# Linear attention and a highway layer on one core: 64-row turns, unequal score and state groups, 512-column feed-forward, buffers behind a pad, a new order

## The chip, the cores and the metric

The kernel runs on one core of one Trainium2 chip. A core has a matrix engine (TensorE, PE in the profile), three engines for elementwise work (VectorE or DVE, ScalarE or ACT, GpSimd or POOL), and SyncE (SP), which here only issues DMAs. TensorE reads SBUF and writes the eight banks of PSUM; the other engines move results from PSUM to SBUF. The metric is the device time of one execution in microseconds (us), lower is better.

## What is computed

Inputs are q, k, v of 4 batches x 8 heads x 768 positions x 64, a decay `lam` per head, and a highway layer (two 512x512 matrices, one bias). First comes linear attention with decay; its output, 3072 tokens of 512 features, goes through the layer.

```python
# attention, per batch and head, in blocks of 64 positions
intra = (qb @ kb.T * Dmask) @ vb            # Dmask[i, j] = lam ** (i - j) for i >= j, else 0
inter = (qb * lam_pow) @ kv_state           # lam_pow[i] = lam ** (i + 1)
out   = intra + inter
kv_state = lam ** 64 * kv_state + (kb * rev_pow).T @ vb
...
# highway layer on x = out, tokens by 512
H = np.maximum(x @ w_h, 0.0)
T = 1.0 / (1.0 + np.exp(-(x @ w_t + b_t)))
return T * H + (1.0 - T) * x
```

The kernel scales q by lam to the power of the position and v by its inverse, so that the decay needs no mask of its own and the state no rescaling: inside a chunk only a triangle of ones is left. T*H + (1-T)*x is computed as x + T*(max(H, 0) - x).

## The kernel before

**Units.** The work is cut into twelve pairs n = 0 to 11 of 2 x 128 positions, three for each batch; a pair has chunks b = 0 and 1 of 128 positions. Positions 2p and 2p+1 lie in partition p (J = 2), so that a DMA row is 512 bytes; a chunk is then one half of the partitions. Heads are handled two at a time (hp = 0 to 3, e = 0 or 1 within).

**An order written out by hand.** `PLAN` is a string of tokens, each of which issues one step. The order of tokens is the order in each engine's queue; the engine stands behind `@`, the PSUM bank behind `=`. Each engine works its queue in order, and the semaphores between engines follow from the tiles. The first pairs' tokens:

```python
Lk.0.0 Lv.0.1 Lv.0.0 Lq.0.0 Lk.0.1 Lq.0.1 Lv.1.1 CK.0.0@POOL Lq.1.0 Z.12=0 TK.0.0=0 Lq.1.1 CV.0.0@DVE Lk.1.0
CQ.0.0@POOL EK.0.0@DVE Lv.1.0 CV.0.1@DVE CK.0.1@ACT Lk.1.1 Z.11=1 TQ.0.0=1 B=2 EQ.0.0@ACT CQ.0.1@POOL W.0.1 W.0.0
```

**The steps of a pair**, with token, function and line:

1. `Lk`, `Lq`, `Lv` load half the heads of k, q or v, 256 KB (L178); `W` loads half a weight matrix, rows of 2 KB (L182). All come from SP's queue, and so do the stores. Five buffers each hold k, q and v.
2. `CK` casts k to bf16 (L102 or L100), `CQ` and `CV` scale q and v by the powers of lam (L195), mostly on POOL.
3. `TK`, `TQ` turn k and q on TensorE, eight turns of 128x128 each (L209), into one bank each. `EK`, `EQ` evacuate them; EQ also interleaves the two positions of a partition (`c j`), so that q stands in the order of positions.
4. `SS` issues, for one e, 16 score matmuls (64x64 tiles, 128 columns, L222) in turn with 16 state matmuls (64 columns, L227). `KE` copies the state out of PSUM. `M` multiplies 512 elements of scores by the triangle on VectorE (L261).
5. `I` (inter, state times q, full array, L277) and `A` (intra, masked scores times v, 64x64 tiles, L287) add up in one bank for each chunk. `D` takes the sum to SBUF as bf16, feature by token: the feed-forward's input xT.
6. `F` is one feed-forward block: eight matmuls of 256 columns (L305), half the output features of one matrix for one pair. A pair has four: u = 0, 1 for w = 0 (H) and w = 1 (T). `H` computes max(H, 0) - x on VectorE (L310), `G` the sigmoid on ScalarE in two instructions of 256 columns (L319), in place in PSUM, `X` the gate on VectorE (L323).
7. `R` adds x and the gated part and turns the sum to token by feature, with 32 matmuls of 64x128 tiles against the identity (L352). `E` copies it to SBUF, `ST` stores 512 KB from SP's queue (L361). The last pair goes in two groups of 128 tokens, with full-array turns (L332) and stores in pieces (L342).

`Z` issues matmuls of 512 columns that nobody reads (spins, L371), to raise TensorE's clock and hold it while data is awaited. `B` and `BC` turn the bias to a column. Before the plan, lam is loaded to all 128 partitions, and its logarithm and powers are computed (L126 to L133). Small tiles (lam_bc, bt_r, id128, blank, tri, the powers and others) are allocated ahead of the weights and the load buffers.

The feed-forward's blocks are independent of the next pairs' attention, so the plan puts them between the attention's steps.

## Time and profile before

| | |
|---|---|
| median of 3 runs | 109.11 us (108.94 to 109.52) |
| span of the profiled execution, first to last instruction | 107.8 us |
| median less span | 1.3 us |
| mean granted TensorE clock | 0.992 |
| read from HBM, written | 20.98 MB, 6.29 MB |
| packets of the load queue | 42528 |

The profile is one execution. A page gives the busy time of each engine, the span in 40 slices, the DMA queues, the chain of work that ended last, the costliest groups and the DMA issues; other views give groups by form, waits, the chain in order of time, windows and the timeline. In a group, "out<-in" are tiles, a leading b marks a PSUM bank, and the last column is the idle time before the instructions with what ended it. Busy time of matmuls includes their latency, so the chain is the better source for their price: there, each piece reaches to the start of the next. Durations below are rounded as the views give them.

### The profile page before, as it was taken

The numbers are of one execution on the slowest core, as the hardware profiler recorded it, in microseconds if no ns is written. First come the engines' busy times: TensorE is split into PE (matmuls) and PEld (weight loads), VectorE is DVE, ScalarE is ACT, GpSimd is POOL, SyncE is SP. The second block draws the span as 40 slices with busy tenths as digits, with TensorE's granted clock in tenths as the row PEclk, the third lists the DMA queues.
The fourth block names the chain that finished last, engine by engine and source line by source line (L and its number), as shares of the span: only waits on it lengthen the run. The fifth ranks groups of instructions, "written<-read, shape, count | busy, mean of one in ns | idle before, by whom it ended". The sixth has DMA issues, their size and how long they took to land.

```text
span 107.8 us, 4970 instructions
## 1 busy us (share of the span) xinstructions
PE 100.5 (93%) x2190; PEld 81.0 (75%) x2190; DVE 83.4 (77%) x140; ACT 70.1 (65%) x129; POOL 55.6 (52%) x46
## 2 busy tenths in 40 slices
PE   4998999999999999999999999999999899999950
PEld 1333655488987888889889889889898688899940
DVE  1053495879699987999995997999977978958860
ACT  2213347485875588499669758957697778587940
POOL 6028342127889887985468593999770600000000
PEclk9999999999999999999999999999999999999996
DMA  1799999999999999999999999999979334108264
GB/s 29 191 304 289 292 356 389 324 292 266 288 288 263 312 295 291 276 291 281 292 298 285 272 360 309 306 289 342 355 220 317 141 138 158 43 6 316 79 239 150
DMA packets 42701, 27.59 MB, mean 256 GB/s; under 512 B 1588, under 2 KB 38712, under 8 KB 42680
## 3 DMA queue, kind: packets, MB, share of 16 engines
q1 hardware_dynamic: 42528, 27.27, 86.7%
q8 instruction: 17, 0.28, 1.1%
q14 instruction: 4, 0.03, 0.1%
q10 hardware_dynamic: 152, 0.01, 0.1%
HBM read 20.98 MB, written 6.29 MB: 253 GB/s over the span
## 4 chain that ended last, share of the span: by engine, by line
PE 74%; DVE 10%; DMA 5%; issue 3%; POOL 1%; SPq 1%; ACT 1%; POOLq 0%; DVEq 0%
PE bt L305 18%; PE bh L305 17%; PE bs L222 7%; PE bx L352 6%; PE bo L287 6%; DMA qf<-in_q_dram 5%; DVE m L261 5%; PE bqtr L209 5%; PE bspin L371 5%; PE bktr L209 4%; PE bo L277 3%; DVE hm L310 2%; DVE th L323 2%; PE kv L227 2%; POOL qb L195 1%
## 5 line engine op out<-in xcount | busy, mean ns | idle before, releaser
L305 PEld LDWEIGHTS <-w_b 128*128 128x128 bf16 x416 | 36.4, 98 | 5.3 <-issue 0.9
L261 DVE TENSOR_TENSOR m<-bs,tri 128x512 bf16<-128x512 f32 x48 | 31.1, 683 | 2.8 <-PE bs L222 2.6
L195 POOL TENSOR_TENSOR qb<-qf,pow_q 128x1024 bf16<-128x1024 f32 (+1 forms) x13 | 23.5, 1810 | 9.4 <-DMA qf<-in_q_dram 8.7
L319 ACT ACTIVATE bt<-bt,bt_col 128x256 f32<-128x256 f32 (+1 forms) x52 | 22.0, 432 | 7.9 <-PE bt L305 4.4
L305 PE MATMUL bt<-xT,w_b 128*128 128x256 bf16 (+1 forms) x208 | 24.5, 265 | 0.7 <-issue 0.5
L305 PE MATMUL bh<-xT,w_b 128*128 128x256 bf16 (+1 forms) x208 | 25.0, 265 | 0.0
L195 POOL TENSOR_TENSOR vs<-vf,pow_v 128x1024 bf16<-128x1024 f32 x10 | 19.0, 1903 | 8.8 <-DMA vf<-in_v_dram 6.4
L310 DVE SCALAR_TENSOR_TENSOR hm<-bh,xT 128x512 bf16<-128x512 f32 (+1 forms) x26 | 16.5, 644 | 3.3 <-PE bh L305 2.4
L323 DVE TENSOR_TENSOR th<-bt,hm 128x512 bf16<-128x512 f32 (+1 forms) x26 | 16.5, 644 | 2.1 <-ACT bt L319 2.0
L371 PE MATMUL bspin<-blank,id 128*128 128x512 bf16 x45 | 13.4, 447 | 1.4 <-POOL id masks.py:199 1.4
L222 PE MATMUL bs<-qT,kT 64*64 64x128 bf16 x384 | 13.9, 218 | 0.4 <-PE bspin L371 0.2
L100 ACT ACTIVATE ss<-kv 128x512 bf16<-128x512 f32 x15 | 9.0, 597 | 7.5 <-PE bs L222 6.3
L102 POOL CAST kb<-kf 128x1024 bf16<-128x1024 f32 (+1 forms) x10 | 9.9, 994 | 6.0 <-DMA kf<-in_k_dram 6.0
L222 PEld LDWEIGHTS <-kT 64*64 64x64 bf16 x384 | 10.9, 106 | 2.6 <-issue 1.1
L100 ACT ACTIVATE xT<-bo 128x512 bf16<-128x512 f32 x16 | 9.2, 597 | 4.4 <-PE bo L287 4.4
L100 ACT ACTIVATE o<-bx 128x512 f32<-128x512 f32 x19 | 10.5, 596 | 1.3 <-PE bx L352 1.3
L100 ACT ACTIVATE qT<-bqtr 128x1024 bf16<-128x1024 bf16 (+1 forms) x10 | 9.8, 980 | 1.8 <-PE bqtr L209 1.8
L371 PEld LDWEIGHTS <-id 128*128 128x128 bf16 x45 | 4.5, 110 | 7.1 <-issue 2.8
L287 PE MATMUL bo<-m,vs 64*64 64x128 bf16 x384 | 9.1, 219 | 0.4 <-DVE m L261 0.4
L227 PE MATMUL kv<-vs,kb 64*64 64x64 bf16 x320 | 9.3, 196 | 0.0
L100 ACT ACTIVATE kT<-bktr 128x1024 bf16<-128x1024 bf16 (+1 forms) x7 | 6.8, 970 | 2.1 <-PE bktr L209 2.1
L287 PEld LDWEIGHTS <-vs 64*64 64x64 bf16 x384 | 6.5, 106 | 2.1 <-issue 1.2
(50 smaller groups left out, 111.1 us busy)
## 6 DMA issues: line engine op xcount, KB each, us to landing
kf<-in_k_dram SPq DMA_DIRECT2D x24, 256.0 KB, 5.3
vf<-in_v_dram SPq DMA_DIRECT2D x24, 256.0 KB, 5.3
qf<-in_q_dram SPq DMA_DIRECT2D x24, 256.0 KB, 5.7
out_dram<-o SPq DMA_DIRECT2D x11, 512.0 KB, 4.8
w_f<-in_moe_w_h_dram SPq DMA_DIRECT2D x2, 512.0 KB, 6.0
w_f<-in_moe_w_t_dram SPq DMA_DIRECT2D x2, 512.0 KB, 8.4
out_dram<-oh SPq DMA_DIRECT2D x2, 128.0 KB, 2.0
out_dram<-oq SPq DMA_DIRECT2D x1, 256.0 KB
```

The source lines that it names most:

```text
L100: A.activation(dst, src, AF.Copy)
L102: ENG[eng].tensor_copy(dst, src)
L195: ENG[eng].tensor_tensor(dst, in0=get(src, n)[:, heads(p)].rearrange("p h (j d) -> p h j d", j=J), in1=pw[:, n % NST, heads(p), :, None].t ...
L222: T.matmul(get("s", n, e, hp // 2)[half(b), hp % 2, j, :], lhsT=get("kT", n)[half(e), hp, j, half(b)], rhs=get("qT", n)[half(e), hp, b * C ...
L227: T.matmul(kv[half(e), hp, half(e)], lhsT=get("kb", n)[half(b), j, 2 * hp + e, :], rhs=get("vs", n)[half(b), 2 * hp + e, j, :], start=firs ...
L261: V.tensor_tensor(new(("m", n, e, u), [128, 2, J, C]), in0=get("s", n, e, u), in1=tri[:, None].to_broadcast([128, 2, J, C]), op=ALU.mult)
L287: T.matmul(get("o", n, b)[half(e), hp, :], lhsT=get("vs", n)[half(b), 2 * hp + e, j, :], rhs=get("m", n, e, u)[half(b), hp % 2, j, :], sta ...
L305: T.matmul(t[:, r, :], lhsT=w_b[w][:, kc, (2 * u + r) * 128:(2 * u + r + 1) * 128], rhs=get("xT", *g)[:, kc, :], start=(kc == 0), stop=(kc ...
L310: V.scalar_tensor_tensor(new(("hm", g, u), [128, 2, z * C], tag=f"hm{z}"), in0=get("h", g, u), scalar=0.0, in1=get("xT", *g)[:, 2 * u:2 * ...
L319: A.activation(dst[:, r, :], src[:, r, :], AF.Sigmoid, bias=bt_col[:, 2 * u + r:2 * u + r + 1])
L323: ENG[eng].tensor_tensor(new(("th", g), [128, NP, z * C], tag=f"th{z}")[:, 2 * u:2 * u + 2, :], in0=get("tt", g, u), in1=get("hm", g, u), ...
L371: T.matmul(t, lhsT=id128, rhs=blank, start=True, stop=True)
```

## The change

- **Turns.** k and q of a pair are turned in 64-row pieces, each chunk into a bank of its own that holds k and q (`turn_kq`, tokens `TK.n.x.p`, x = 0 for k and 1 for q); an evacuation takes one chunk, k and q together or one of them (`evac_kq`, token `E`). The interleave moves from q to the evacuation of the attention output (`take`), and the triangle is laid out accordingly.
- **Scores.** For each e, 8 scores stand with 16 states (`SU`), and the other 16 scores of both e in a step of their own (`S`).
- **Feed-forward.** `GROUPS` gives the groups: pairs 0, 1 and 10 alone (256 columns), 2+3, 4+5, 6+7, 8+9 together (512 columns), and the two chunks of pair 11 alone (128). A block has one PSUM bank of 512 columns; a group of 512 has eight blocks, four for each matrix. The sigmoid of such a block is one instruction. With `@POOL` it writes to SBUF and POOL computes the gate (13 of 25), with `@DVE` it stays in PSUM.
- **lam** is loaded as one row; its logarithm is spread over the partitions by a matmul (`powers`). The bias's turn is the first token.
- **Buffers** are all allocated at the start, behind a tile of 384 bytes, and each has a multiple of 512 bytes. Load buffers are six instead of five, output buffers three instead of five.
- **Order.** The plan is new. Weights are loaded in halves of columns (rows of 1 KB), the first behind 18 loads of q, k and v, where before it stood behind 12; three stores instead of five stand ahead of the last load. Pair 11's turns follow pair 10's directly. Spins are 26 instead of 45. The last pair's chunks come last, one stored in two pieces of 128 KB, the other as 256 KB.

```diff
+GROUPS = [[(0, 0), (0, 1)], [(1, 0), (1, 1)], [(2, 0), (2, 1), (3, 0), (3, 1)], [(4, 0), (4, 1), (5, 0), (5, 1)], [(6, 0), (6, 1), (7, 0), (7, 1)], [(8, 0), (8, 1), (9, 0), (9, 1)], [(10, 0), (10, 1)], [(11, 0)], [(11, 1)]]
...
+B=0 L.0.0.0 L.1.0.0 L.1.0.1 Z.3.512=1 PW=1 CQ.0.1@POOL L.2.0.1 Z.7.512=2 TK.0.1.1=12 PT L.0.0.1 CK.0.0@ACT TK.0.0.0
...
+D.0.0@DVE SU.1.1=6 W.0.1 W.1.1 KE.1.0@ACT WC.0.1.1@POOL E.2.1.1@ACT M.1.1.0 M.1.0.1 Z.3.512=4 SU.1.0=1 I.1=64 L.1.3.1
...
+CQ.11.2@POOL S.9=51 M.9.1.1 M.9.0.1 D.8.0@ACT D.8.1@ACT TK.10.0.2=46 L.2.11.0 TK.10.1.2 CK.11.2@POOL KE.9.0@ACT
+TK.11.0.2=12 TK.11.1.2 E.11.0.2@ACT E.10.1.2@DVE E.10.0.2@DVE CV.10.2@POOL SU.9.0=5 KE.9.1@ACT M.9.0.0 ST.3.2.2
...
+R.11.1.0=56 X.8.0.1@DVE H.7.0.2 R.11.1.1=03 ER.11.1.1.1@ACT ER.11.1.0.0@ACT ER.11.1.1.0@ACT ST.11.1.1 X.7.0.2@DVE
+ER.11.1.0.1@DVE ST.11.1.0 R.11.0.2=40 ER.11.0.2.1@ACT ER.11.0.2.0@DVE ST.11.0.2
...
-BUFS = dict(kf=5, qf=5, vf=5, kb=3, qb=2, vs=3, kT=2, qT=2, m=8, xT4=2, th4=2, xT2=3, xT1=2, th2=2, th1=2, hm2=3, hm1=2, tb2=2, tb1=2, ss=4, o=5, oh=2, oq=1)
+BUFS = {'kf': 6, 'qf': 6, 'vf': 6, 'o': 3, 'oh': 1, 'oq': 2, 'kb': 3, 'qb': 2, 'vs': 3, 'kq': 3, 'm': 10, 'ss': 4, 'hm': 3, 'tb': 3, 'x128': 2, 'x256': 2, 'x512': 2, 't128': 2, 't256': 2, 't512': 2}
...
-    lam_bc = singles.tile([128, H], F32)
-    A.dma_start(out=lam_bc, in_=lam.partition_broadcast(128))
+    pad = singles.tile([128, 96], F32)
+    ln_r = pad[0:1, 0:H]
+    bt_col = pad[:, 8:8 + KC]
...
+    for tag in BUFS:
+        for i in range(BUFS[tag]):
+            kept[tag, i] = singles.tile(*SHAPES[tag], name=f"{tag}_{i}_")
...
+    A.dma_start(out=lam_r, in_=lam.rearrange("(o h) -> o h", o=1))
...
+    def powers(bk):
+        ln = bank(("ln",), bk[0], [128, H])
+        T.matmul(ln, lhsT=ones, rhs=ln_r, start=True, stop=True)
+        V.tensor_tensor(p_ln, in0=ln[:, None, :, None].to_broadcast([128, NST, H, J]),
+                        in1=tk_f[:, :, None, :].to_broadcast([128, NST, H, J]), op=ALU.mult)
+        A.activation(pow_q, p_ln, AF.Exp)
+        A.activation(pow_v, p_ln, AF.Exp, scale=-1.0)
...
-    def load_w(w, g):
-        nc.sync.dma_start(out=w_f[w][:, 2 * g:2 * g + 2],
-                          in_=(moe_w_h, moe_w_t)[w][256 * g:256 * g + 256].rearrange("(kc p) m -> p kc m", p=128))
...
+    def load_w(w, c):
+        cs = slice(256 * c, 256 * c + 256)
+        nc.sync.dma_start(out=w_f[w][:, :, cs], in_=(moe_w_h, moe_w_t)[w][:, cs].rearrange("(kc p) m -> p kc m", p=128))
...
+    def turn_kq(n, x, p, bk):
+
+        for b in range(2):
+            bank(("kqt", n, b), bk[b] if bk else 0, [128, 2, NP, J, Q], BF16)
+        for hp in range(NP) if p == 2 else (2 * p, 2 * p + 1):
             for j in range(J):
-                T.transpose(t[:, i, j, :], get(x + "b", n)[:, j, h:h + 2, :], id128)
...
+                for b in range(2):
+                    T.transpose(get("kqt", n, b)[:, x, hp, j, :], get(("kb", "qb")[x], n)[half(b), j, 2 * hp:2 * hp + 2, :],
+                                id128[half(b), half(b)])
+
+    def evac_kq(n, b, x, eng):
+
+        xs = slice(0, 2) if x == 2 else slice(x, x + 1)
+        copy(eng, new("kq", n)[:, b, xs], get("kqt", n, b)[:, xs])
...
     def scores_state(n, e, bk):
...
+        bank(("s", n, e, 0), bk[0], [128, 2, J, J, Q])
+        with_state = e == 1 or n % NST != NST - 1
+        for i, (hp, j) in enumerate(PJ[:4]):
+            for b in range(2):
+                score(n, e, hp, j, b)
+            if with_state:
+                for hp, j in PJ[2 * i:2 * i + 2]:
+                    for x in range(2):
+                        state(n, 1 - e, hp, j, x)
...
     def take(n, b, eng):
...
+        g, at = place[n, b]
+        copy(eng, new(f"x{width[g]}", g)[:, :, at:at + C].rearrange("p n (c j) -> p n j c", j=J),
+             get("ob", n, b).rearrange("p n (j c) -> p n j c", j=J))
...
+    def block(g, u, w, bk):
+        z = width[g]
+        r = 512 // z
+        t = bank(("HT"[w], g, u), bk[0], [128, r, z])
+        for i in range(r):
             for kc in range(KC):
...
+                T.matmul(t[:, i, :], lhsT=w_b[w][:, kc, (r * u + i) * 128:(r * u + i + 1) * 128],
+                         rhs=xt(g)[:, kc, :], start=(kc == 0), stop=(kc == KC - 1))
...
+    def sigm(g, u, p, eng):
...
+        if eng == "POOL":
+            made["S", g, u] = new("tb", g, u).rearrange("p (r z) -> p r z", z=z)
+        else:
+            made["S", g, u] = t
+        for i in range(s.start, s.stop):
+            A.activation(get("S", g, u)[:, i, :], t[:, i, :], AF.Sigmoid, bias=bt_col[:, r * u + i:r * u + i + 1])
...
+    def gate(g, u, p, eng):
...
+        ENG[eng].tensor_tensor(new(f"t{z}", g)[:, r * u + s.start:r * u + s.stop, :], in0=get("S", g, u)[:, s],
+                        in1=get("hm", g, u).rearrange("p (r z) -> p r z", z=z)[:, s], op=ALU.mult)
...
-    def spin(r, bk, idle=[0]):
+    def spin(r, z, bk, idle=[0]):
```

## The prediction

> **What bounds the kernel now.** I read the page first, then the chain, the waits, the windows by stage and the groups by form. The page gives the busy shares, the slices and the chain:

> ```profile
> span 107.8 us, 4970 instructions
> ## 1 busy us (share of the span) xinstructions
> PE 100.5 (93%) x2190; PEld 81.0 (75%) x2190; DVE 83.4 (77%) x140; ACT 70.1 (65%) x129; POOL 55.6 (52%) x46
> ...
> PE   4998999999999999999999999999999899999950
> ...
> DMA  1799999999999999999999999999979334108264
> ...
> PE 74%; DVE 10%; DMA 5%; issue 3%; POOL 1%; SPq 1%; ACT 1%; POOLq 0%; DVEq 0%
> ```

> TensorE is full from the second slice to the 38th and holds 74% of the chain. But a second row is as full: the DMA engines up to slice 31. The waits and the timeline of POOL say what that means:

> ```profile
> POOL qb L195 <- DMA qf<-in_q_dram: 8.7, 7, 2.1
> POOL vs L195 <- DMA vf<-in_v_dram: 6.4, 3, 4.1
> POOL kb L102 <- DMA kf<-in_k_dram: 6.0, 5, 3.0
> ```
> ```profile
> 84.43 1.90 POOL L195 TENSOR_TENSOR vs<-vf,pow_v 128x1024 bf16<-128x1024 f32 x1 [4.08 <-DMA vf<-in_v_dram]
> ```

> POOL waits for loads until the last V, 84.4 us into the span. TensorE has some 2 us of other work when each pair of chunks lands; a TensorE that gets faster by several us runs into the loads. So two paths have to be summed: TensorE's own, and the load stream. The windows give the stream's rate (columns: length, busy of each engine, clock, DMA share, GB/s):

> ```profile
> 14.00:20.00 6.00, 5.53 (x107) 3.28 (x101) 4.50 (x7) 3.20 (x4) 1.93 (x3) 1.00 1.06 375
> 20.00:58.00 38.00, 37.76 (x907) 32.32 (x900) 33.48 (x54) 27.98 (x50) 27.06 (x18) 1.00 1.07 288
> ```

> In 20 to 58 us only q, k and v move, in rows of 512 bytes: 288 GB/s. In 14 to 20 us nearly all is weights, in rows of 2 KB: 375 GB/s. With 16 engines a row of 512 bytes takes 16x512/288 = 28.4 ns and one of 2 KB 87.4 ns, so 512 bytes more cost 19.7 ns and each row has a fixed 8.8 ns.

> **The change on TensorE.** Prices come from the chain (start, us, what):

> ```profile
> 15.91 1.74 PE bspin L371 x8
> ...
> 34.00 0.57 PE bx L352 x32
> 34.58 0.55 PE bqtr L209 x8
> 35.13 0.87 PE bt L305 x8
> ...
> 40.21 0.45 PE bktr L209 x8
> ...
> 41.75 0.57 PE bo L287 x32
> ```

> Eight turns of 128 rows take 0.45 us after other full-array work and 0.55 after 64-row work: a full matmul of 128 columns is 56 ns, and a change between full, 64x128 and 64x64 tiles about 0.10 us (0.093 by the unrounded starts). Thirty-two 64-row matmuls take 0.57 with one such change, so 0.47, or 14.7 ns each, both for 64x128 (L352) and for 64x64 tiles (L287). A matmul of 256 columns is 0.87/8 = 109 ns, one of 512 columns 1.74/8 = 217 ns, and two of the first are one of the second.

> - Turns: 192 full ones (10.8 us) become 384 of 64 rows; their form, 64 rows by 128 with 64 columns, is that of L352, so 384 x 14.7 ns = 5.6 us: 5.1 less.
> - Scores and states: the same 384 and 320 matmuls, in groups of 24 and 16: 10.9 becomes 10.6.
> - Feed-forward: the same columns, in matmuls of 512 for four groups: 42.1 becomes 41.8. Eight steps instead of four for twice the tokens is no gain in itself.
> - Output turns 6.1 becomes 5.6; inter 4.5 and intra 5.4 stay.
> - Tile changes: counted along both plans, 59 become 68: 5.5 becomes 6.3, as each 64-row turn now interrupts full-array work.

> Together 85.3 us of needed TensorE work becomes 80.1. What stands behind the first feed-forward block falls from 79.2 to 72.2, since pair 2 is turned and scored ahead of it now (work ahead of it: 6.1 becomes 7.9, beside the spins, 45 becoming 26, which lie in time that waits for data anyway).

> The same sum against the trace of before:

> ```profile
> 5.65 0.61 POOL L102 CAST kb<-kf 128x512 bf16<-128x512 f32 x1 [3.00 <-DMA kf<-in_k_dram]
> ...
> 22.24 1.91 PE L305 MATMUL bh<-xT,w_b 128*128 128x256 bf16 x16
> ```
> ```profile
> 104.34 0.42 DVE L102 COPY oh<-bx 128x256 f32<-128x256 f32 x1 [0.44 <-PE bx L332]
> ```

> From 22.2 to 104.3, where the last copy gets its data from TensorE, are 82.1 us for 79.2 of work: 2.9 of stalls. Behind that come 3.5 us of evacuation and store.

> **The other engines.** These rows price them (groups by form of VectorE, ScalarE and POOL; then the load of lam, with its time to landing):

> ```profile
> L261 DVE TENSOR_TENSOR m<-bs,tri 128x512 bf16<-128x512 f32 x48 | 31.1, 683 | 2.8 <-PE bs L222 2.6
> ...
> L102 DVE COPY kT<-bktr 128x1024 bf16<-128x1024 bf16 x5 | 3.4, 685 | 1.2 <-PE bktr L209 1.1
> L102 DVE CAST ss<-kv 128x512 bf16<-128x512 f32 x5 | 3.4, 681 | 0.0
> L102 DVE COPY qT<-bqtr 128x1024 bf16<-128x1024 bf16 x2 | 2.4, 1224 | 0.4 <-PE bqtr L209 0.4
> ```
> ```profile
> L319 ACT ACTIVATE bt<-bt,bt_col 128x256 f32<-128x256 f32 x44 | 19.5, 449 | 7.7 <-PE bt L305 4.4 <-ACT xT L100 1.8 <-ACT o L100 0.8
> L100 ACT ACTIVATE o<-bx 128x512 f32<-128x512 f32 x19 | 10.5, 596 | 1.3 <-PE bx L352 1.3
> ```
> ```profile
> L195 POOL TENSOR_TENSOR qb<-qf,pow_q 128x1024 bf16<-128x1024 f32 x11 | 20.9, 1902 | 7.1 <-DMA qf<-in_q_dram 6.4 <-PE bx L352 0.7
> ...
> L195 POOL TENSOR_TENSOR qb<-qf,pow_q 128x512 bf16<-128x512 f32 x2 | 2.6, 1303 | 2.3 <-DMA qf<-in_q_dram 2.3
> L102 POOL CAST w_b<-w_f 128x512 bf16<-128x512 f32 x3 | 1.8, 625 | 5.8 <-DMA w_f<-in_moe_w_h_dram 3.4 <-DMA w_f<-in_moe_w_t_dram 2.5
> ```
> ```profile
> lam_bc<-in_lam_dram ACTq DMA_DIRECT2D x1, 4.0 KB, 4.4
> ```

> - VectorE: the interleave leaves the turned q (1224 against 685 ns) for the evacuation of the attention output, which reads 4-byte PSUM at 683 ns in any order (as the masks and the state copies do). Thirteen gates go to POOL, some output and state evacuations change sides with ScalarE. Counted along the plan, about 82 us against 83.4.
> - ScalarE: 16 sigmoids of 512 columns at about 0.60 (the row of o) replace two of 0.45 each: 22 becomes 17.6; copies and casts of k take that up: about 68.
> - POOL: 13 gates of 128x512, which the trace does not show on POOL. Ends: 0.95 (half the 1902 row) and 1.30 (the mean of two of 512 elements). I take 1.04, nearer to the half, which has 11 instances behind it. 55.6 becomes about 63.
> - Behind the first block VectorE has 68.5 us, ScalarE 58, POOL 51.5 against TensorE's 72.2. But up to pair 6 it is VectorE 35.4 and POOL 32.6 against 34.9: no slack there. One evacuation now takes k and q of a chunk together, so it waits for the later of the two, as a rule POOL's scaling of q, 1.9 us behind its load; the masks and gates queued behind it on VectorE wait with it, and TensorE's intra part for those. I put the stalls at 3.5 us, 0.6 over those of before: less than one such wait of 1.9, as the plan puts feed-forward blocks between.
> - lam as a row: the first scalings of q waited 2.3 us for their data and not for the powers, so nothing is won. Deeper load buffers (six instead of five) win nothing by themselves either: the DMA share is over 1 already. The bias turn is first in TensorE's queue now and everything there waits for its small load, up to about 5 us; the lam load, its neighbour, took 4.4. Only spins stand behind it: nothing, at most 1 us.

> **The load stream.** The new pad of 384 bytes stands first, and every buffer behind it has a multiple of 512 bytes; before, small tiles of 3584 bytes in sum (seven times 512) stand there with no such pad, so if the pad brings the buffers onto a 512-byte boundary, all load buffers lie 128 bytes past one now. No row of the trace has an aligned transfer. The bounds: nothing (28.4 ns a row, 288 GB/s), or the whole fixed part (19.7 ns); the fastest stage seen, 375, lies between. I take half, 24 ns or 340 GB/s; the other rows at 375. (The weights come in rows of 1 KB now; between the two, 0.1 us each.)

> [...]

> The first block waits for the first half of one weight matrix, which now stands behind 18 loads (4.72 MB) instead of ahead of most of pair 2: 5.65 (the first load, above) + 4.46/0.340 + 0.52/0.375 + two casts of 0.625 on POOL = 21.4 us. At 288 it is 23.8.
> The last k half stands behind 18.6 MB of loads and 3.67 MB of weights and stores (three stores of 0.52 instead of five ahead of it): 5.65 + 18.35/0.340 + 9.8 = 69.4 us. Its cast takes 1.0, and from the last turns on TensorE has 26.2 us left.
> The end: behind the last block come relu and gate (0.68 each, as a mask), 16 turns (0.24) and a copy of 0.42, with about 0.1 from engine to engine 2.5 us; 0.6 of it (the turns that the plan has there) is in TensorE's sum already. Then a store of 256 KB instead of 128: 3.0 us follow the copy at 104.34 (which ends at 104.76) up to 107.8, and 128 KB more are 0.35 at 375 GB/s. Together 5.3 us behind TensorE's sum, where before had 3.5.

> **Sums.** TensorE's path: 21.4 + 72.2 + 3.5 + 5.3 = 102.4. Load path: 69.4 + 1.0 + 26.2 + 5.3 = 101.9. They are as good as equal, and the first sets the end. Median 109.11 less the span 107.8 leaves 1.3 around it: **103.7 us**, 5% less than before.

> **Rivals.**
> - *The loads run no faster.* Then the load path decides: 5.65 + 63.7 + 9.8 + 32.5 = 111.7, and 113.0 us: slower, since the new order puts all of pair 11's turns late and together. It decides against the change below 307 GB/s (18.35/r = 107.8 - 47.95). For it: rows of 512 bytes run at 288 now, and their fixed part may have nothing to do with where they start. Against: 2 KB rows show that neither memory nor engines are at their limit at 288.
> - *VectorE and POOL take over up to pair 6.* With gates at 1.30 to 1.56 POOL gets 2 to 3 us more work there than fits, and in-order queues hand it on: stalls of 7, 107.2 us. For it: VectorE is busy 33.5 of 38 us in the window from 20 to 58. Against: before had 34.8 of 36.3 there too, with 2.9 of stalls in all.
> - *The 64-row turns don't overlap* (the change doesn't do what it says): 29 ns each instead of 14.7, 5.6 us back: 109.3. Against it: L352's pairs with the same shape.
> - *Loads as fast as the weights*, 375: the first block at 20.2, 102.5, or 101 with fewer stalls.

> **Chances.** Forecast 0.60 (its own range 101.5 to 106), loads unchanged 0.15, VectorE and POOL 0.15, turns 0.05, faster loads 0.05. The range 101.0 to 109.6 leaves out the first rival and little else; half-way loads (307 to 325 GB/s) lie in it. About 0.5% is what a measurement of this kernel can tell from no change. Faster: forecast, VectorE/POOL and fast loads, 0.78 with what falls off at their edges; same: half of the turns and an edge of VectorE, 0.04; slower: the loads and half of the turns, 0.18.

> **What would show it.** In the profile after: a window with q, k and v alone at about 340 GB/s, not 288; the DMA row falling off near slice 27 of 40; turns of 16 in about 0.24 us; first block near 21.4; POOL's waits on loads no longer than now; TensorE's last matmul near 99. Wrong it would be if the last casts of k and v wait for DMA past 75 us, if POOL's gates take over 1.3, or if TensorE idles on masks and gates for over 5 us.

## The result, and the profile after

The kernel takes 114.64 us (median of four runs, 113.97 to 117.33) against 109.31 before on the same chip: a ratio of 1.0431, 95% interval 1.0341 to 1.0521. It is 4% slower; 103.7 us, and faster, was forecast. Ratios, and the single times given below, leave out disturbed runs, which were 2 to 7 us longer and up to three of the four of one kernel (in e4 two of four, 114.73 and 114.85 us); the traces of e2 and e8 are of such runs.

The page of the kernel after, profiled at 113.97 us:

```profile
span 112.3 us, 5101 instructions
PE 94.8 (84%) x2253; PEld 62.8 (56%) x2253; DVE 80.6 (72%) x137; ACT 68.1 (61%) x116; POOL 65.0 (58%) x58
...
PE   0699879849999999999899986299999999999920
...
PEclk9999999995999999999999999959999999999996
DMA  2999999999999999999999999993200000081783
...
q8 instruction: 17, 0.28, 1.0%
...
PE 69%; DVE 10%; issue 7%; DMA 7%; ACT 3%; ACTq 0%; DVEq 0%
```

TensorE was 93% of the span and is 84%. The loads end at slice 27, as forecast. VectorE, ScalarE and POOL came out at 80.6, 68.1 and 65.0 us, against 82, 68 and 63 forecast. New are two holes in TensorE's row (slices 9 and 25 to 26), two 5s in the granted clock just behind them, and "issue", time in which an engine waits for nothing that the profile shows: 7% of the chain instead of 3%.

The windows after (same columns as before):

```profile
14.00:20.00 6.00, 5.02 (x164) 3.30 (x163) 4.62 (x10) 4.10 (x9) 5.09 (x7) 1.00 1.09 327
20.00:58.00 38.00, 35.02 (x868) 24.46 (x868) 30.83 (x51) 26.88 (x42) 29.13 (x22) 0.96 1.06 314
```

The loads run at 314 GB/s: above 288, below 340. A tenth of that is weights, in rows of 1 KB; from 32 to 56 us, where q, k and v are alone, it is 307 (289 before). TensorE loses 3 of 38 us where it lost 0.2. The chain says at what:

```profile
22.14 1.73 issue
23.88 0.22 PE bs L233
24.19 0.23 PE bob L302 x14
24.42 1.20 PE bH L328 x8
25.61 3.20 PE bT L328 x16
...
60.48 0.57 PE bkqt L224 x32
...
68.37 1.06 PE bot L372 x61
69.43 2.92 issue
72.35 0.23 PE bot L372 x3
72.58 1.55 PE bH L328 x4
74.13 1.71 PE bT L328 x4
75.84 1.13 PE bH L328 x4
```

Read the long stop first. It stands between the 61st and the 62nd of 64 output turns (pairs 4 and 5, L372). The three turns behind it read the same two buffers, write the same banks and run on the same engine as those ahead; no data can be missing. The stop at 22.14 is of the same kind, within a group of scores and states. Behind both, feed-forward matmuls run at half speed for a while: four of 512 columns take 1.55 and 1.71 us instead of 0.87, sixteen of 256 take 3.20 instead of 1.74. That is where the clock row has its 5s (granted clock 0.50 from 25.1 to 28.4 and from 72.9 to 76.2 us); the two places cost some 1.8 us each.

Counted in the trace in order of start, a weight load and a matmul for each of the 2253, such stops stand ahead of instructions 700, 2236, 2748 and 3004 (from 0): 1536, 512 and 256 apart, all multiples of 256. The instruction queue of the DMA (q8 above) moved 17 packets of 16 KB for these 4506 instructions, which fits 256 to a packet. From the start of the last matmul ahead of a boundary of 256 to that of the first behind it are, over all boundaries, 7.3 us in sum (1.93, 0.19, 0.85, 0.74 and 3.11, and small ones in which TensorE doesn't stop), against 1.3 before the change; the idle time alone is 5.8 us (1.73, 0.64, 0.52 and 2.92).

The packets' times tie the two together. In the trace after, TensorE goes on 1.44, 1.49, 1.36 and 1.34 us after a packet of the instruction queue has landed. At every boundary where the packet had landed 1.69 us ahead or more, there is no stop. A packet's transfer starts 0.7 to 3.4 us after TensorE has crossed the boundary before, and in one case 0.46 us ahead of it.

### The profile page after: what moved, and what is told of

It is laid out like the page before. It is cut to its first block, busy times and chain, and to the rows that moved or that the text cites. A ratio compares the mean times of both kernels' runs of the same rounds, so it can differ in the third digit from the quotient of the medians.

```text
span 112.3 us, 5101 instructions
## 1 busy us (share of the span) xinstructions
PE 94.8 (84%) x2253; PEld 62.8 (56%) x2253; DVE 80.6 (72%) x137; ACT 68.1 (61%) x116; POOL 65.0 (58%) x58
## 4 chain that ended last, share of the span: by engine, by line
PE 69%; DVE 10%; issue 7%; DMA 7%; ACT 3%; ACTq 0%; DVEq 0%
PE bT L328 18%; PE bH L328 16%; PE bs L233 8%; PE bspin L401 7%; PE bob L302 5%; DMA out_dram<-o__87 5%; PE bot L372 5%; PE bkqt L224 4%; PE bob L292 4%; DMA bt_r<-in_moe_b_t_dram 2%; PE kv L238 2%; DVE hm__119 L339 2%; DVE hm__118 L339 2%; ACT bT L352 1%; DVE m__109 L272 1%
## 5 line engine op out<-in xcount | busy, mean ns | idle before, releaser
L328 PEld LDWEIGHTS <-w_b 128*128 128x128 bf16 x288 | 25.2, 102 | 16.1 <-issue 2.8
L352 ACT ACTIVATE bT<-bT,pad 128x128 f32<-128x128 f32 (+2 forms) x20 | 9.3, 469 | 12.1 <-PE bT L328 6.3
L328 PE MATMUL bT<-x__127,w_b 128*128 128x512 bf16 x32 | 9.1, 412 | 0.0
L328 PE MATMUL bH<-x__127,w_b 128*128 128x512 bf16 x32 | 8.9, 410 | 0.0
L401 PE MATMUL bspin<-blank,id 128*128 128x512 bf16 x26 | 8.8, 454 | 0.0
L328 PE MATMUL bH<-x__128,w_b 128*128 128x512 bf16 x32 | 8.1, 379 | 0.0
L328 PE MATMUL bT<-x__128,w_b 128*128 128x512 bf16 x32 | 8.0, 380 | 0.0
L107 ACT ACTIVATE x__128<-bob 128x512 bf16<-128x512 f32 x8 | 5.7, 751 | 1.6 <-PE bob L302 1.4
L233 PE MATMUL bs<-kq__102 64*64 64x128 bf16 x128 | 4.4, 221 | 1.7 <-issue 1.7
L233 PE MATMUL bs<-kq__101 64*64 64x128 bf16 x128 | 4.8, 220 | 0.8 <-issue 0.6
L233 PE MATMUL bs<-kq__100 64*64 64x128 bf16 x128 | 4.8, 220 | 0.5 <-DVE kq__100 L109 0.5
L372 PE MATMUL bot<-id,x__128 64*128 64x64 bf16 x64 | 2.3, 191 | 3.3 <-issue 2.9
L328 PE MATMUL bT<-x__125,w_b 128*128 128x256 bf16 x32 | 5.0, 310 | 0.0
L233 PEld LDWEIGHTS <-kq__100 64*64 64x64 bf16 x128 | 3.2, 106 | 3.2 <-issue 2.1
L233 PEld LDWEIGHTS <-kq__101 64*64 64x64 bf16 x128 | 3.4, 106 | 2.6 <-issue 1.8
L233 PEld LDWEIGHTS <-kq__102 64*64 64x64 bf16 x128 | 3.2, 106 | 3.0 <-issue 2.7
L352 ACT ACTIVATE tb__122<-bT,pad 128x512 bf16<-128x512 f32 x4 | 2.7, 685 | 3.3 <-PE bT L328 3.3
L107 ACT ACTIVATE kq__101<-bkqt 128x1024 bf16<-128x1024 bf16 (+1 forms) x5 | 4.3, 856 | 0.8 <-PE bkqt L224 0.7
L107 ACT ACTIVATE kq__100<-bkqt 128x1024 bf16<-128x1024 bf16 (+1 forms) x3 | 2.7, 892 | 3.3 <-PE bkqt L224 3.3
```

What stands on the lines that cost most here:

```text
L107: A.activation(dst, src, AF.Copy)
L233: T.matmul(get("s", n, e, hp // 2)[half(b), hp % 2, j], lhsT=get("kq", n)[half(e), b, 0, hp, j, :], rhs=get("kq", n)[half(e), b, 1, hp], s ...
L328: T.matmul(t[:, i, :], lhsT=w_b[w][:, kc, (r * u + i) * 128:(r * u + i + 1) * 128], rhs=xt(g)[:, kc, :], start=(kc == 0), stop=(kc == KC - 1))
L352: A.activation(get("S", g, u)[:, i, :], t[:, i, :], AF.Sigmoid, bias=bt_col[:, r * u + i:r * u + i + 1])
L372: T.matmul(get("ot", n, c, p, e)[:, a, k, :], lhsT=x[half(e), j, at:at + C], rhs=id128[half(e), half(e)], start=(a == 0 and k == 0 and i = ...
L401: T.matmul(t, lhsT=id128, rhs=blank[:, 0:z], start=True, stop=True)
```

## Experiments

Theory: **code**. TensorE's instructions come in blocks of 256, one ahead, as the packets' times above suggest. Where a block is done sooner than the next can come, TensorE stops, and the granted clock falls behind a long stop (0.50 behind those of 1.73 and 2.92 us; it goes along with them, see the end of the next section). Rivals: a **wait** that the profile doesn't name; the **store** near the end, which is the longest piece of the chain; the **alignment** or the **order** of the loads.

**Moving the blocks (e1).** 64 instructions more among the first spins.

```diff
-B=0 L.0.0.0 L.1.0.0 L.1.0.1 Z.3.512=1
+B=0 L.0.0.0 L.1.0.0 L.1.0.1 Z.32.8=1 Z.3.512=1
```

> 32 matmuls of 8 columns (64 instructions of TensorE) more among the first spins, nothing else. Theory 'code': TensorE's stops of 1.73 us at 22.1 and of 2.92 us at 69.4 stand at the ends of blocks of 256 instructions (16 KB of the instruction queue each), so with 64 instructions more ahead of them every stop moves 64 instructions back in the program: the long one falls after about 29 of the 64 turns of the output of pairs 4 and 5 instead of after 61, or wherever that block now ends; the stops are again 1536, 512 and 256 instructions apart. Time within 1.5 us of 114. Rival 'wait': TensorE waits there for a buffer, a bank or a gate, and the stop stays between the 61st and the 62nd turn.

114.45 us. The chain of this kernel:

```profile
68.52 0.59 PE bot L372 x29
69.11 2.37 issue
71.48 0.70 PE bot L372 x35
72.18 1.82 PE bH L328 x4
```

The stop now stands behind the 29th turn, 64 instructions earlier in the program, and ahead of instruction 3004 again; the two others of over 0.5 us stand ahead of 700 and 2236 again. A wait for data would have stayed with its turn. "Wait" falls.

**The supply measured by itself (e7).** TensorE alone, with turns of 64 rows, in three stages: without transfers, beside loads, beside stores.

```diff
+    turns(x, 256)
+    ... 40 loads of 256 KB ...
+    turns(y, 320)
+    ... 12 stores of 512 KB ...
+    turns(z, 256)
```

> No part of the reference's work: TensorE alone does 512, 640 and 512 turns of 64 rows (1024, 1280 and 1024 instructions); the first without any transfer, the second beside 40 loads of 256 KB in rows of 512 bytes, the third beside 12 stores of 512 KB in rows of 2 KB; zeros and a corner of a load are stored. Theory 'code': a block of 256 such instructions is 1.9 us of work, but a block can't follow the one before it faster than 3 to 3.3 us without transfers, 4.4 to 5.7 beside the loads and as much or more beside the stores. Rival: the stops come from something else in the kernel after the change, and all turns run at 14.7 ns each, 1.9 us a block, in all three parts.

The chain in the stage without transfers, and TensorE's timeline in the two others (128 turns are 256 instructions):

```profile
6.55 0.24 issue
6.79 2.04 PE p L124 x128
8.83 1.41 issue
10.24 2.04 PE p L124 x128
12.29 1.96 issue
14.24 0.69 PE p L124 x33
```
```profile
23.89 3.60 PE L124 MATMUL p<-id,y 64*128 64x64 bf16 x128 [3.60 <-issue]
28.17 3.60 PE L124 MATMUL p<-id,y 64*128 64x64 bf16 x128 [0.68 <-issue]
33.27 3.27 PE L124 MATMUL p<-id,y 64*128 64x64 bf16 x128 [1.50 <-issue]
38.09 0.65 PE L124 MATMUL p<-id,y 64*128 64x64 bf16 x33 [1.56 <-issue]
...
62.17 2.04 PE L124 MATMUL p<-id,z 64*128 64x64 bf16 x128 [1.20 <-issue]
67.27 3.33 PE L124 MATMUL p<-id,z 64*128 64x64 bf16 x128 [3.06 <-issue]
72.37 0.65 PE L124 MATMUL p<-id,z 64*128 64x64 bf16 x33 [1.77 <-issue]
```

Every stop stands behind exactly 128 turns. From block to block it takes 3.45 and 4.00 us without transfers (3 to 3.3 expected), 4.28, 5.10 and 4.82 beside the loads (the first block beside them, which ends at 23.89, took 6.19), 5.10 twice beside the stores. The work of a block is 2.04 us, 3.3 to 3.6 where the clock has fallen (mean 0.62 of full speed beside the loads, where TensorE does nothing else than run and stop). So beside the loads TensorE gets 41 to 60 instructions per us, and a 64-row turn uses two in 14.7 ns. The longest of these stops is 3.60 us. In the stops shown TensorE goes on 1.25 to 1.64 us after a packet of the instruction queue has landed, as in the kernel.

**Fewer instructions, more work (e4).** Full turns for keys and queries again, all else as after.

```diff
-                for b in range(2):
-                    T.transpose(get("kqt", n, b)[:, x, hp, j, :], get(("kb", "qb")[x], n)[half(b), j, 2 * hp:2 * hp + 2, :],
-                                id128[half(b), half(b)])
+                T.transpose(get("kqt", n, x)[:, hp, j], get(("kb", "qb")[x], n)[:, j, 2 * hp:2 * hp + 2, :], id128)
```

> The turns of keys and queries are full ones again (192 of 128 rows instead of 384 of 64), with the buffers, the order and everything else as after the change. Theory 'code': TensorE's own work grows by 5.1 us, but 384 instructions less are 1.5 blocks less; stops at block ends fall from 7.1 us to under 3, and the half clock after them goes too: 112 to 115 us, no slower than after the change. Rival 'work': TensorE is the bound by its work, and 5 us of it come back: 118 to 120.

110.05 (profiled) and 110.52 us, better than either theory had it: with 5.1 us of work (by the prediction's prices) put back on TensorE the kernel is 4 us faster, though on these two runs alone. From start to start the boundaries fall to 2.2 us in sum, one of them 0.81; TensorE's waits (total, number, longest) have one entry without a releaser:

```profile
PE kv L238 <- issue: 0.6, 1, 0.6
```

**The same instructions in another order (e5).** Output turns of pairs 4 and 5 behind feed-forward blocks.

```diff
-R.4.2.2=53 M.8.1.0 ... R.5.2.2=14 F.4.1.0=0 ... F.4.1.1=3 ... F.4.3.0=5 ... I.8=20 F.4.0.0=4 ...
+M.8.1.0 ... F.4.1.0=0 ... F.4.1.1=3 ... F.4.3.0=5 H.4.3.2 R.4.2.2=61 ... I.8=20 F.4.0.0=4 ... A.8.1 ... R.5.2.2=54
```

> Only the order changes: the output turns of pairs 4 and 5 (128 instructions, with their evacuations and other banks) stand behind two to four of the feed-forward blocks of the next group instead of ahead of them. As many instructions, as much work. Theory 'code': the blocks of 256 instructions that now follow each other within 2.5 to 5 us are drawn out by 3.4 us of work with 32 instructions; the stops at 66 and 69 us (0.74 and 2.92) and the half clock behind them (some 1.8 us) shrink by 2.5 to 4.5 us in sum, and the time by about as much, to 110 to 112. Rival 'loads': TensorE then waits for k, q or v of pairs 10 and 11 instead, and less than 1 us is won.

111.64 us, 1.0231 of before (1.0148 to 1.0314): 2 points better than the kernel after. No stop at a boundary is left between 57 us and the end, and the clock row is all 9s. Not all of that is the new order's: the stop at 22.14, which it doesn't touch, is 1.03 us in this trace and 1.73 after. TensorE's waits without a releaser, after (first three rows) and in e5:

```profile
PE bot L372 <- issue: 2.9, 1, 2.9
PE bs L233 <- issue: 2.4, 2, 1.7
...
PE bob L302 <- issue: 0.5, 1, 0.5
```
```profile
PE bs L234 <- issue: 2.0, 2, 1.0
```

**Is the new order better in itself? (e9)** e5's order on full turns.

> Full turns for all keys and queries, the output turns of pairs 4 and 5 behind the next feed-forward blocks, and five output buffers. Theory 'code': with 384 instructions less there is next to nothing left for the new order to win: the one stop of 0.82 us at 66 us of the kernel with full turns goes, 109 to 110.3 us (110.05 and 110.52 without the new order). Rival 'order': the new order is better for reasons of its own, and wins here what it won with 64-row turns, 2.5 to 3 us: 107 to 108.

111.75 us, 1.0182 (1.0105 to 1.0259): the order wins nothing without stops to remove, it even seems to cost about 1 us (against e4's two runs, on another chip), more than "code" said. "Order" as a gain of its own falls. TensorE's waits in e9 have two that e4's lack:

```profile
PE bH L329 <- DVE kq__102 L110: 0.7, 1, 0.7
PE bkqt L224 <- POOL qb__97 L209: 0.5, 1, 0.5
```

The same two stand in e5, 0.8 and 0.5 us, so there the new order pays them out of what the missing stops give. The five output buffers, which e4 and e5 don't have, were not tried by themselves on full turns.

**Both at once (e8).** e5's order, five output buffers, and full turns for five pairs (`FULL = (0, 1, 2, 8, 9)`).

> The order of the kernel with the output turns of pairs 4 and 5 behind feed-forward blocks, and full turns of 128 rows for pairs 0, 1, 2, 8 and 9, where instructions are densest (160 turns and 320 instructions less, 2.1 us more work for TensorE), and five output buffers. Theory 'code': the stops at block ends together under 3 us (7.1 after the change), 107 to 110 us. Rival 'work': the added 2.1 us come on top, 113 to 116.

111.70 and 112.47 us, 1.0263 (1.0155 to 1.0371): neither theory's number. The boundaries had moved, and stops stood in other dense places: 1.83 us within output turns at 52, 1.25 within states at 66, 0.93 at 79.

**The store at the end (e2).** The chain after has "98.28 5.28 DMA out_dram<-o__87": ScalarE waits for a store to free its buffer.

```diff
-'o': 3
+'o': 5
```

> Five buffers for whole output pairs instead of three, nothing else. Theory 'store': the 5.3 us near the end in which ScalarE waits for the store out of the buffer that it wants (o of pair 6, landed at 103.6) go, and with them ScalarE's gates of the last groups come earlier: 109.5 to 111 us, 3.5 to 5 less than 114.6, and the stops of TensorE stay as they are. Rival 'TensorE': the last groups are late because TensorE was late by then, the wait is hidden by other waits: less than 1 us.

The four runs spread from 112.01 to 117.66 (median 114.66); the times decide nothing. The trace, with the granted clock at 1.00 from 84 to 102 us as after the change, does: from the start of the 64 output turns (95.63 after) to the sigmoids (104.08) were 8.45 us with the wait; without it they are 8.26 (99.52 to 107.78):

```profile
99.52 1.04 PE bot L372 x64
...
106.68 1.02 PE bT L328 x16
...
107.78 0.35 ACT bT L352
```

TensorE is busy there until the sigmoids' block is done, wait or no wait. The longest piece of the chain was worth 0.2 us in this stretch: "store" falls.

**Alignment (e3, e6).** A pad of 512 bytes, which shifts the load buffers by 128 bytes (by the tiles' sizes 128 past a multiple of 512 again; the traces have no addresses); and the pad alone in the kernel before.

```diff
-    pad = singles.tile([128, 96], F32)
+    pad = singles.tile([128, 128], F32)
```

> The pad is 512 bytes instead of 384, so that all load buffers lie 128 bytes past a multiple of 512 again, as before the change. Theory 'alignment': the rate of q, k and v from 20 to 58 us falls from 314 to about 288 GB/s, and the kernel, which then waits for loads until 80, becomes 2 to 5 us slower. Rival 'order': the rate does not hang on the place (the median packet of 512 bytes took 27 ns before and after), 314 stays, and the time is within 1 us of 114.6.

1.0601 (1.0532 to 1.0671) against 1.0431: slower by 1.7 points, a little under the 2 us expected, and the window from 20 to 58 us falls from 314 to 291 GB/s (298 to 318 in e1, e2, e4, e5, e8 and e9, with the pad of 384):

```profile
20.00:58.00 38.00, 34.16 (x884) 23.97 (x871) 29.84 (x49) 27.53 (x43) 28.97 (x21) 0.96 1.04 291
```

In the kernel before (one unused tile ahead of all others):

```diff
+    pad = singles.tile([128, 96], F32)
     lam_bc = singles.tile([128, H], F32)
```

> The kernel before the change with one unused tile of 384 bytes a partition ahead of all others, so that its load buffers lie on multiples of 512 bytes; nothing else. Theory 'alignment': the window from 20 to 58 us, where the DMA engines are full, shows 305 to 320 GB/s instead of 288; TensorE is the bound there, so the time falls by 0 to 1.5 us. Rival 'order': 288 stays and the time is the same within 0.5%.

108.55 us, 0.9902 (0.9856 to 0.9949): **this version beats both kernels**, the one before by 1%. The window from 5 to 14 us, first in the kernel before, then here:

```profile
5.00:14.00 9.00, 8.50 (x104) 4.21 (x101) 4.01 (x8) 2.41 (x6) 4.35 (x4) 1.00 1.18 298
```
```profile
5.00:14.00 9.00, 8.54 (x113) 4.56 (x114) 5.74 (x10) 3.16 (x8) 4.65 (x4) 1.00 1.13 350
```

298 becomes 350 GB/s; from 20 to 58 us it is only 293, nearer to "order" than to the 305 to 320 of "alignment", though the mean of a 512-byte packet falls there from 30.2 to 27.9 ns. The rate alone is no measure of the place: from 32 to 56 us, with q, k and v alone, it is 307 GB/s after, 279 in e3, 289 before and 282 in e6, at DMA shares of 1.05, 1.01, 1.08 and 0.98; e6 has the faster packets and doesn't fill the engines with them. Over the whole run the mean is 30.1 ns before and in e3, and 27.4 to 27.8 in the eight kernels with the pad of 384; the median is 27 in all.

## Why the prediction was wrong

**Held.** The 64-row turns overlap: 32 in 0.57 us with one tile change, as priced (60.48 above). The loads run faster for their place in memory (291 GB/s with it shifted by 128 bytes, in e3), though half as much as taken or less: 314, and 307 for q, k and v alone (26.7 ns a row by the prediction's reckoning, not 24). The 340 was a choice between two bounds; no run shows it from 20 to 58 us (288 to 318). The weights for the first block were cast at 21.9 us, 21.4 forecast (20.73 + 1.17 below). What stands behind TensorE's sum took 5.6 us (106.7 to 112.3) against 5.3. POOL's gates take 1.15 us (1.04 taken, 0.95 to 1.30 as bounds). POOL's timeline and its groups:

```profile
20.73 1.17 POOL L109 CAST w_b<-w_f 128x512 bf16<-128x512 f32 x2 [0.38 <-DMA w_f<-in_moe_w_h_dram]
...
74.64 1.04 POOL L109 CAST kb__94<-kf__73 128x1024 bf16<-128x1024 f32 x1 [0.20 <-DMA kf__73<-in_k_dram]
```
```profile
L358 POOL TENSOR_TENSOR t__134<-tb__120,hm__119 128x512 bf16<-128x512 bf16 x2 | 2.3, 1154 | 3.0 <-ACT tb__120 L352 3.0
```

**Failed: TensorE's path, 21.4 + 72.2 + 3.5 + 5.3.** Two terms were too small, mainly for one reason: the sum had no term for the supply of instructions.
- The first block came at 24.4, not 21.4. Its weights were there at 21.9; TensorE was late by a stop of 1.73 us. The rest of the 3.0 is not accounted for.
- "Stalls 3.5" became 10.1: from 24.4 to 106.7 (the last feed-forward matmul ends at 106.48, and 0.24 of turns follow) are 82.3 us, of which 72.2 are the work as priced. 4.9 us are stops at block boundaries (0.19, 0.85, 0.74 and 3.11, from start to start), about 3.6 the half clock at the two places shown, and 1.6 remain for all the waits for which I had set 3.5.

24.4 + 72.2 + 10.1 + 5.6 = 112.3, the span. (The work after the change, 80.1, is 79.8 by the terms listed; nothing hangs on it.) The error lies in the step "384 x 14.7 ns = 5.6 us: 5.1 less". It took matmuls to cost only their time. That price came from groups of 32, shorter than a block, and each turn was two instructions. 192 turns more are 1.5 blocks more, in a stream that before the change ran 3840 instructions in 79.7 us (21.3 to 101.0), 48 per us, where e7 had 41 to 60 beside loads. The prediction says of feed-forward in eight steps that it "is no gain in itself"; by instructions it is one, since as many columns take fewer of them. So TensorE has only 63 matmuls more in all (2253, 2190 before), and e5 shows with the same number that it matters how closely the short ones follow each other. Before the change no block of 256 that ran beside loads took less than 4.5 us, and one stop stood among them (0.53 us idle); after it, the blocks ahead of the stops at 22.1, 55.6, 66.2 and 69.4 took 3.41, 3.97, 4.26 and 2.54.

**The load path** stayed second, but its rate was over-estimated too: the last k was cast at 74.6 and not 69.4. At 314 GB/s the prediction's own sum gives 5.65 + 18.35/0.314 + 9.8 + 1.0 + 26.2 + 5.3 = 106.4, and 107.7 us with the 1.3 around it. From the last k's own time it is 74.6 + 1.0 + 26.2 + 5.3 = 107.1, and 108.4 us. So, by these estimates, without any stop the kernel would have come to about 108, hardly faster than before and not to 103.7; the rate by itself would not have made it slower. No run shows it: the best with the changes, e4, took 110.05.

**The rivals** named loads, VectorE with POOL, and turns that don't overlap. None is what happened, and none of the three signs of being wrong came (the last k was cast at 74.6, POOL's gates took 1.15, TensorE waited 1.1 us for a gate and 0.4 for masks): the slower side was reached through a resource that the list of engines and queues in the prediction didn't hold. It could have been seen: the third part of the page of before has the instruction queue, and the trace of before has one stop of 0.74 us at a boundary, between turns and a feed-forward block.

```profile
q8 instruction: 17, 0.28, 1.1%
```

What stays open: how much of the half clock would stay without stops was not tried by itself, it only goes along with them (the profiles of e4 and e5 have 9s up to the last slice, e3 kept 9s behind a stop of 2.45 us, and e5's fastest run, 111.33, had a mean clock of 0.970); and why the aligned rate is 350 in the first window of the kernel before, but 314 after.

## What to carry to other kernels

Count TensorE's instructions as well as its columns: a matmul is two (4506 for 2253 here), and where 256 of them took less than 4 to 5 us while loads ran, the engine could stop for the rest (beside the loads of e7 a block came every 4.28 to 5.10 us; after the change a block of 2.54 us was followed by 2.92 of stop). Cutting a matmul in two by its rows doubles the instructions and can cost more than it saves (whole turns: 110.05 and 110.52 us in e4, against 114.64); spread such groups among long matmuls (111.64 in e5), or leave them whole. A piece of the chain that waits is worth only what the next latest thing leaves of it.

## What the runs showed of the hardware that was not expected

```profile
L107 ACT ACTIVATE x__128<-bob 128x512 bf16<-128x512 f32 x8 | 5.7, 751 | 1.6 <-PE bob L302 1.4
```
